# Fourth and fifth key-weight pieces by DMA transposes on two queues

## The chip, the cores and the metric

The kernel runs on one core of a Trainium2 chip. The metric is the device time of one execution in microseconds (us); the figure compared is the median of the timed runs. One further execution is taken under the hardware profiler, and the profile and the trace come from it.

## What is computed

The reference is one transformer layer over 2048 tokens of width 640: layer normalisation, linear attention with 32 heads of width 20, and a SiLU feed-forward part of width 1728, each with its residual. The change touches only the keys. Cut to what matters:

```python
x = A_x                                             # 1 x 2048 x 640, bf16
qkv = layernorm(x) @ wqkv                           # 640 x 1920: q, k, v
pk = einsum("bhsd,hdf->bhsf", k, w_phi)             # per head, 20 x 20
phi_k = concat([softmax(pk), softmax(-pk)])         # likewise phi_q from q
kv, z = sum over tokens of phi_k * v, phi_k
h = x + (phi_q @ kv / (phi_q @ z + 1e-6)) @ wo
out = h + silu(layernorm(h) @ w1) @ w2
```

Since the head map `w_phi` follows directly on the key projection, the kernel multiplies the two weights once (`Wfk` = key weights times the block-diagonal `w_phi`) and then projects each token tile with `Wfk`. For that product TensorE needs the key weights transposed: the tile `wTk`.

## The kernel before

The tokens lie in 16 tiles of 128. The width 640 is cut in C = 5 pieces of 128, and so are the key weights: piece c is rows 128c to 128c + 127 of the key columns. Persistent tiles hold the tokens (`X`), the weights, and the results in between; PSUM is one tile `mm` of eight banks, and the number behind `@` in the order is the bank that a step writes.

The order of all work is written out by hand in the string `ORDER`: each word is a step (`wt.3` is the function `op_wt(3)`), and each engine and each DMA queue takes its own instructions strictly in the order in which the words give them. A tile framework puts in the waits between engines. Two queues issue DMAs: SP (SyncE), which does nothing else, and ACT (ScalarE), which also computes. In the steps for loads a last letter `a` means ACT and `s` means SP.

The steps around the change, with their lines in the profile:

- `lx.a.b` loads token tiles a to b - 1 into `X`, `lk.a.b` key pieces a to b - 1 into `wk`, `lv.a.b` value pieces into `wv`, `lo.a.b` output weights, `lp` the head map (all issued at L236).
- `wm.n` are matmuls on constants ahead of the first data (L268).
- `wt.c` transposes key piece c on TensorE, five 128 x 128 transposes into PSUM (L322); `wc.c` copies the result into `wTk`, on VectorE (L169) or ScalarE (L171).
- `fk.c` multiplies piece c of `wTk` with the head map (six matmuls, L337), `fc.c` copies the product to `Wfk`, on ScalarE (L171).
- `st.t` takes the statistics of token tile t on VectorE (L273, L274), `rs` turns them into scale and offset on GpSimd, `xn.t` normalises (L297 on VectorE, L302 on ScalarE), `xt.t` transposes the tile on TensorE (L308) and `xc.t` copies it, for tiles 0 to 3; for the other twelve `xd.t` does both by a DMA transpose on SP (L315).
- `kp.t` and `vp.t` project token tile t with `Wfk` and with `wv` (ten matmuls each, L370; the pieces 0 to 4 are read one after the other).
- `ta` loads ScalarE's table for the exponential (L264).
- `lq.c` brings a piece of the query weights transposed by a DMA transpose on SP (L251). The step `lt.c` (L254) does the same for a key piece, and the order of before doesn't use it.

In the order of before SP issues: token tile 1, key pieces 0 to 3 one by one, then X[2:4], X[8:12], value pieces 0 to 2, value pieces 3 and 4, X[4:8], X[12:16], output weights. ACT issues X[0:1], the head map and key piece 4 and then goes on to compute. TensorE's order in the opening is `wm`, `wt.0`, `wm`, `wt.1`, `fk.0`, `wt.2`, `wt.3`, `fk.1`, `fk.2`, `wt.4`, `fk.3`, `xt.0`, `fk.4`, `xt.1`, `kp.0`, `kp.1`, `vp.1`, `xt.2`, `vp.0`, `vp.2`, `xt.3`, `kp.2`, `kp.3`.

Of the kernel before, what the change touches and what calls it, by code (L numbers as in the profile page):

```python
# [22 lines left out]
WHERE = {t: (g, i) for g, ts in enumerate(GROUPS) for i, t in enumerate(ts)}  # L23

ORDER = """
mk mo lx.0.1.a lk.0.1.s lp.a lx.1.2.s lk.4.5.a wm.512@7 wm.512@7 wm.512@7 wm.512@7 wm.512@7 wm.512@7
wm.512@7 wm.512@7 wt.0@0 lk.1.2.s ta wc.0.a wm.256@2 wm.256@2 wm.256@2 wm.256@2 wm.256@2 wm.256@2 wt.1@1 wc.1.a st.0 rs.0.1
ph.v fk.0@2 fc.0.a st.1 lk.2.3.s wt.2@4 wc.2.v lk.3.4.s wt.3@5 wc.3.v fk.1@6 fc.1.a rs.1.2 fk.2@0 fc.2.a
lx.2.4.s xn.0.v lx.8.12.s wt.4@4 wc.4.v lv.0.3.s fk.3@2 fc.3.a xt.0@5 xn.1.v xc.0.v st.2 fk.4@6 fc.4.a
rs.2.3 lv.3.5.s mc.0 xt.1@4 xc.1.a st.9 st.8 rs.8.10 lx.4.8.s st.3 rs.3.4 kp.0@0 ke.0 xn.2.a kp.1@2 ke.1  # L30
lx.12.16.s vp.1@6 st.10 xt.2@5 vp.0@0 xc.2.a xn.9.a vc.0.a vp.2@2 st.11 lo.2.5.s xn.3.v xt.3@4 xc.3.a
rs.10.12 xn.8.a vc.2.a vc.1.a kp.2@0 ke.2 st.4 xd.9 st.5 kp.3@4 lo.0.2.s ke.3 rs.4.6 vp.3@2 xn.11.v vp.9@6
# [38 lines left out]
def kernel(  # L71
# [11 lines left out]
    nc = tc.nc  # L83

    P = nc.NUM_PARTITIONS
    T = 16
    D = 640
# [46 lines left out]
    wTk = first.tile([P, C, D], BF16, name="wTk")  # L134
# [116 lines left out]
        nc.sync.dma_start_transpose(wTq[:, :, c * P : (c + 1) * P], A_wqkv[c * P : (c + 1) * P, 0:D])  # L251

    def op_lt(c, q="s"):
        nc.sync.dma_start_transpose(wTk[:, :, c * P : (c + 1) * P], A_wqkv[c * P : (c + 1) * P, D : 2 * D])  # L254

    def op_lo(a, b, q="s"):
        dma(q, wo[:, a:b, :], A_wo[a * P : b * P].rearrange("(c p) n -> p c n", p=P))
# [500 lines left out]
```

## Time and profile before

| what | us |
|---|---|
| timed runs, median of 3 | 236.51 (236.49 to 236.56) |
| the profiled execution | 236.35 |
| its span, first to last instruction | 234.4 |
| TensorE busy | 230.5 (98%) |
| VectorE busy | 133.5 (57%) |
| ScalarE busy | 114.5 (49%) |
| GpSimd busy | 95.4 (41%) |

The span lies within the profiled execution; the 1.95 us between them are before the first and after the last instruction. In the profile's rows PE is TensorE, DVE VectorE, ACT ScalarE, POOL GpSimd; SPq and ACTq are the DMA issues of a queue. `out<-in` names the tiles written and read, xN is the number of instructions in a row, and all times count from the start of the span.

### The profile page before, as it was taken

Reading aid. Unit: us, or ns where it says so; the run is one execution under the profiler, and the core shown is the slowest. Engines: PE = TensorE matmul, PEld = TensorE weight load, DVE = VectorE, ACT = ScalarE, POOL = GpSimd, SP = SyncE. Lnnn points to the kernel's source line nnn. Section 1 sums busy time; section 2 is a strip of 40 time slices with the busy share of each in tenths; the row PEclk is TensorE's granted clock in tenths of the full one; section 3 lists DMA queues with packets and bytes.
Section 4 is the critical chain, followed back from the end, with each engine's and each line's share of the span. In section 5 each row is a group of like instructions: output and inputs, shape, how many; then the busy total and the mean of one; then the engine's idle time right before and its main releaser. Section 6 shows DMA issues by size and latency. Waiting matters only on the chain.

```text
span 234.4 us, 6307 instructions
## 1 busy us (share of the span) xinstructions
PE 230.5 (98%) x2674; PEld 148.4 (63%) x2674; DVE 133.5 (57%) x249; ACT 114.5 (49%) x171; POOL 95.4 (41%) x190
## 2 busy tenths in 40 slices
PE   8999999999999999999999999999999999999995
PEld 4777777776554556876645455556776865566662
DVE  3999999999968899788956641301341310001132
ACT  3789996885857776742244536260040015613000
POOL 7485798997904455765285123141040000000000
PEclk9999999999999999999999999999999999999999
DMA  7967758839101375325823202123212300000112
GB/s 203 381 234 147 82 112 110 182 64 350 37 3 31 59 176 148 59 49 98 142 55 61 56 3 55 30 57 63 88 24 57 106 27 5 0 3 2 54 34 81
DMA packets 44844, 20.67 MB, mean 88 GB/s; under 512 B 34448, under 2 KB 44304, under 8 KB 44816
## 3 DMA queue, kind: packets, MB, share of 16 engines
q1 hardware_dynamic: 43728, 19.88, 36.1%
q10 hardware_dynamic: 1088, 0.39, 0.8%
q8 instruction: 21, 0.34, 0.6%
q14 instruction: 7, 0.06, 0.1%
HBM read 9.61 MB, written 2.62 MB: 52 GB/s over the span
## 4 chain that ended last, share of the span: by engine, by line
PE 98%; ACT 1%; DVE 0%; issue 0%
PE mm L691 24%; PE mm L645 24%; PE mm L370 19%; PE mm L457 10%; PE mm L566 9%; PE mm L504 3%; PE mm L268 2%; PE mm L427 2%; PE mm L337 1%; PE mm L655 1%; PE mm L704 1%; ACT EqT L479 1%; PE mm L322 1%; PE mm L308 0%; DVE ob L721 0%
## 5 line engine op out<-in xcount | busy, mean ns | idle before, releaser
L691 PE MATMUL mm<-w,shT 128*128 128x320 bf16 (+2 forms) x416 | 58.7, 299 | 0.0
L645 PE MATMUL mm<-HnT,w 128*128 128x512 bf16 (+1 forms) x325 | 58.6, 337 | 0.0
L691 PEld LDWEIGHTS <-shT 128*128 128x128 bf16 x416 | 39.6, 98 | 17.2 <-issue 1.1
L667 ACT ACTIVATE shT<-mm 128x1024 bf16<-128x1024 f32 (+2 forms) x29 | 27.6, 963 | 44.6 <-PE mm L645 43.1
L712 DVE TENSOR_TENSOR ob<-mm,X 128x640 bf16<-128x640 f32 x15 | 12.3, 819 | 62.3 <-PE mm L691 59.3
L645 PEld LDWEIGHTS <-w 128*128 128x128 bf16 x325 | 31.4, 98 | 23.2
L370 PEld LDWEIGHTS <-XnT 128*128 128x128 bf16 x320 | 30.8, 98 | 12.0
L414 POOL TENSOR_TENSOR Ek<-Ek,Sk 128x1280 bf16<-128x1280 bf16 (+2 forms) x15 | 32.9, 2217 | 4.0 <-DVE Sk L406 4.0
L539 POOL TENSOR_TENSOR o<-u,rd 128x320 bf16<-128x320 f32 x28 | 19.9, 727 | 22.9 <-DVE rd L533 16.4
L583 ACT ACTIVATE sq<-X 128x640 bf16<-128x640 bf16 x16 | 11.7, 732 | 28.3 <-DVE X L575 27.2
L566 PE MATMUL mm<-wo,ot 128*128 128x320 bf16 x160 | 23.9, 299 | 0.3 <-ACT EqT L479 0.3
L457 PE MATMUL mm<-XnT,Wfq 128*128 128x512 bf16 x100 | 23.8, 380 | 0.0
L370 PE MATMUL mm<-wv,XnT 128*128 128x320 bf16 x160 | 23.7, 299 | 0.0
L370 PE MATMUL mm<-Wfk,XnT 128*128 128x320 bf16 x160 | 23.5, 299 | 0.0
L395 ACT ACTIVATE Ek<-mm 128x640 bf16<-128x640 f32 x32 | 20.5, 714 | 6.0 <-PE mm L370 5.1
L403 DVE TENSOR_REDUCE Sk<-Ek 128x64 f32<-128x1280 bf16 x16 | 23.2, 1452 | 0.3 <-ACT Ek L395 0.3
L479 ACT ACTIVATE EqT<-mm 128x1024 bf16<-128x1024 f32 (+1 forms) x24 | 19.7, 879 | 4.9 <-PE mm L457 4.8
L575 DVE SCALAR_TENSOR_TENSOR X<-mm,X 128x640 bf16<-128x640 f32 x16 | 13.0, 818 | 15.4 <-PE mm L566 15.1
L566 PEld LDWEIGHTS <-ot 128*128 128x128 bf16 x160 | 15.7, 98 | 7.3 <-issue 0.2
L273 DVE BATCH_NORM_STATS2 stats<-X 128x6 f32<-128x320 bf16 x32 | 13.6, 467 | 3.8 <-DMA X<-in_A_x_dram 3.8
L457 PEld LDWEIGHTS <-Wfq 128*128 128x128 bf16 x100 | 9.1, 98 | 9.3
L525 DVE TENSOR_TENSOR u<-mm,w 128x672 f32<-128x672 f32 x16 | 13.7, 857 | 1.2 <-DVE w L523 0.3
(78 smaller groups left out, 204.3 us busy)
## 6 DMA issues: line engine op xcount, KB each, us to landing
out_dram<-ob SPq DMA_DIRECT2D x15, 160.0 KB, 1.8
w<-in_B_w_dram SPq DMA_DIRECT2D x6, 360.0 KB, 4.5
X<-in_A_x_dram SPq DMA_DIRECT2D x3, 640.0 KB, 7.8
w<-in_B_w_dram SPq DMA_DIRECT2D x5, 320.0 KB, 5.8
wk<-in_A_wqkv_dram SPq DMA_DIRECT2D x4, 160.0 KB, 4.2
wv<-in_A_wqkv_dram SPq DMA_DIRECT2D x1, 480.0 KB, 6.4
wo<-in_A_wo_dram SPq DMA_DIRECT2D x1, 480.0 KB, 9.7
w<-in_B_w_dram SPq DMA_DIRECT2D x1, 480.0 KB, 4.6
```

The costliest lines, as they stand in the source:

```text
L370: nc.tensor.matmul(ps[:, half, 0:320], tok(XnT[t // GT], t)[:, c, :], W[:, c, half * 320 : (half + 1) * 320], start=(c == 0), stop=(c == C ...
L395: nc.scalar.activation(Ek[:, s, :].rearrange("p (a n) -> p a n", a=2), tl["kp", t][:, :, 0:320], AF.Exp, scale=1.0 - 2.0 * s,)
L403: nc.vector.tensor_reduce(Sk[:], tl["ek", t][:].rearrange("p s (h f) -> p (s h) f", f=DH), axis=AX.X, op=ALU.add,)
L414: nc.gpsimd.tensor_tensor(Ek3[:, 0:n], Ek3[:, 0:n], Sk[:, 0:n].unsqueeze(2).to_broadcast([P, n, DH]), op=ALU.mult,)
L457: nc.tensor.matmul(tl["qp", g, i][:, k, :], Wfq[:, c, r * P : (r + 1) * P], XnT[g][:, c, :], start=(c == 0), stop=(c == C - 1),)
L479: nc.scalar.activation(E[:, s, rs[0] : rs[-1] + 1, :], tl["qp", g, i][:, 0 : len(rs), :], AF.Exp, scale=1.0 - 2.0 * s,)
L525: nc.vector.tensor_tensor(u[:], A[1][:, :, :, 0:21], w[:].unsqueeze(3).to_broadcast([P, 4, 8, 21]), op=ALU.mult,)
L539: (nc.vector if eng == "v" else nc.gpsimd).tensor_tensor(tl["o", t][:, a * 320 : (a + 1) * 320].rearrange("p (h f) -> p h f", f=DH), tl["u ...
L566: nc.tensor.matmul(ps[:, half, 0:320], tl["ot", t][:, c, :], wo[:, c, half * 320 : (half + 1) * 320], start=(c == 0), stop=(c == C - 1),)
L645: nc.tensor.matmul(ps[:, i * W : (i + 1) * W], w1[:, c, fc * P : (fc + 1) * P], HnT[g][:, c, 0:W], start=(c == 0), stop=(c == C - 1), skip ...
L667: nc.scalar.activation(sh[:, a:b], tl["up", g, k][:, 0 : b - a], AF.Silu)
L691: nc.tensor.matmul(ps, shT[g][:, fc * W + i * P : fc * W + (i + 1) * P], w2[:, fc, a:b], start=first and fc == 0, stop=last and fc == FC - ...
```

## The change

The fourth and the fifth key piece (c = 3 and 4) are no longer loaded into `wk`, transposed by `wt` and copied by `wc`. Instead `lt.4` on ACT's queue and `lt.3` on SP's queue bring them from DRAM by DMA transposes straight into their columns of `wTk`, in the places of the order where `lk.4.5.a` and `lk.3.4.s` stood. The step `lt` gets a choice of queue. With the loads go two `wt` steps (ten TensorE transposes) and two `wc` steps (two VectorE copies); all other steps stay as they are and in the same order.

```diff
-mk mo lx.0.1.a lk.0.1.s lp.a lx.1.2.s lk.4.5.a wm.512@7 wm.512@7 wm.512@7 wm.512@7 wm.512@7 wm.512@7
+mk mo lx.0.1.a lk.0.1.s lp.a lx.1.2.s lt.4.a wm.512@7 wm.512@7 wm.512@7 wm.512@7 wm.512@7 wm.512@7
 wm.512@7 wm.512@7 wt.0@0 lk.1.2.s ta wc.0.a wm.256@2 wm.256@2 wm.256@2 wm.256@2 wm.256@2 wm.256@2 wt.1@1 wc.1.a st.0 rs.0.1
-ph.v fk.0@2 fc.0.a st.1 lk.2.3.s wt.2@4 wc.2.v lk.3.4.s wt.3@5 wc.3.v fk.1@6 fc.1.a rs.1.2 fk.2@0 fc.2.a
-lx.2.4.s xn.0.v lx.8.12.s wt.4@4 wc.4.v lv.0.3.s fk.3@2 fc.3.a xt.0@5 xn.1.v xc.0.v st.2 fk.4@6 fc.4.a
+ph.v fk.0@2 fc.0.a st.1 lk.2.3.s wt.2@4 wc.2.v lt.3.s fk.1@6 fc.1.a rs.1.2 fk.2@0 fc.2.a
+lx.2.4.s xn.0.v lx.8.12.s lv.0.3.s fk.3@2 fc.3.a xt.0@5 xn.1.v xc.0.v st.2 fk.4@6 fc.4.a
 rs.2.3 lv.3.5.s mc.0 xt.1@4 xc.1.a st.9 st.8 rs.8.10 lx.4.8.s st.3 rs.3.4 kp.0@0 ke.0 xn.2.a kp.1@2 ke.1
...
     def op_lt(c, q="s"):
-        nc.sync.dma_start_transpose(wTk[:, :, c * P : (c + 1) * P], A_wqkv[c * P : (c + 1) * P, D : 2 * D])
+        (nc.sync if q == "s" else nc.scalar).dma_start_transpose(wTk[:, :, c * P : (c + 1) * P], A_wqkv[c * P : (c + 1) * P, D : 2 * D])
```

## The prediction

> **What bounds the kernel now.** I began with the share of busy time and with the chain of waits, because a small change to the opening is only worth what it takes off that chain. The page says that TensorE (PE) has practically no idle time, and the chain says where its first microseconds go (start, length, instructions; L322 transposes pieces of the key weights, L337 folds them, L308 transposes tokens, L370 projects):
>
> ```profile
> PE 230.5 (98%) x2674; PEld 148.4 (63%) x2674; DVE 133.5 (57%) x249; ACT 114.5 (49%) x171; POOL 95.4 (41%) x190
> 7.02 0.56 PE mm L322 x10
> 7.58 0.80 PE mm L337 x12
> 8.37 0.28 PE mm L322 x5
> 8.65 0.32 PE mm L337 x6
> ...
> 10.04 4.19 PE mm L370 x30
> 14.24 0.28 PE mm L308 x5
> 14.52 2.72 PE mm L370 x20
> 17.23 0.28 PE mm L308 x5
> ```
>
> The reader is to see two things. The transposes that go are on this chain: `wt.2` and `wt.3` together take 0.56 us, `wt.4` 0.28 us. And from 10.04 us on PE runs one matmul after the other, 30 of them in 4.19 us, so a late arrival there is paid in full and nothing later gives it back.
>
> The second view is the timeline of the two issuing queues, SP (SyncE) and ACT (ScalarE), for the opening:
>
> ```profile
> 1.74 1.49 SPq L236 DMA_DIRECT2D wk<-in_A_wqkv_dram  x3
> 3.83 0.80 SPq L236 DMA_DIRECT2D X<-in_A_x_dram  x2
> 4.88 0.93 SPq L236 DMA_DIRECT2D wv<-in_A_wqkv_dram  x2
> ...
> 1.70 0.56 ACTq L236 DMA_DIRECT2D wk<-in_A_wqkv_dram  x1
> 2.28 1.28 ACT L264 ACT_TABLE_LOAD   x1 [2.28 <-issue]
> ...
> 4.97 0.69 ACT L171 COPY wTk<-mm 128x640 bf16<-128x640 bf16 x1 [1.20 <-PE mm L322]
> ```
>
> The third load of the first row is the fourth key piece; behind it on SP stand the token tiles X[2:4] and X[8:12] (both in the row at 3.83) and the whole of the value weights (4.88). The fifth key piece is issued on ACT at 1.70.
>
> The third view is the list of DMA issues with the time from issue to landing (last column), asked for the opening and for a few single issues:
>
> ```profile
> wv<-in_A_wqkv_dram SPq DMA_DIRECT2D x1, 480.0 KB, 6.4
> ...
> X<-in_A_x_dram SPq DMA_DIRECT2D x1, 320.0 KB, 4.0
> wv<-in_A_wqkv_dram SPq DMA_DIRECT2D x1, 320.0 KB, 6.8
> ...
> wk<-in_A_wqkv_dram ACTq DMA_DIRECT2D x1, 160.0 KB, 4.3
> X<-in_A_x_dram SPq DMA_DIRECT2D x1, 640.0 KB, 5.7
> wo<-in_A_wo_dram SPq DMA_DIRECT2D x1, 320.0 KB, 3.3
> L251 SPq DMA_TRANSPOSE wk<-in_A_wqkv_dram x5: 1219/1232/1275, 21.7 to 41.6; - x5
> ...
> DMA to landing us min/median/max: 2.8/3.1/4.2
> ```
>
> From these come the landings of before: X[2:4] at 3.83 + 4.0 = 7.8 us, X[8:12] (issued about 4.25) at 10.0, the first three value pieces at 4.88 + 6.4 = 11.3, the last two (issued about 5.35) at 12.15. The last two rows belong to L251, which brings the query weights later by the same kind of transpose, out of the same array and in the same size: the issuing queue is held 1.23 us and the data stand 2.8 to 4.2 us after the issue, 3.1 in the median.
>
> **The change part by part.** *What PE loses.* `wt.3` is half of the 0.56 us and `wt.4` is 0.28, so 0.56 us leave the chain if everything else is ready. Not all of that can be had: the folds between them also wait for copies. I take 0.5 us as the most that the change can bring.
>
> *What the vector engine loses.* Two copies out of PSUM:
>
> ```profile
> L169 DVE COPY wTk<-mm x3: 480/490/491, 7.3 to 8.7; 128x640 bf16<-128x640 bf16 x3
> ```
>
> That is 2 x 0.49 us, before 9.2 us. It lets the first two normalised tiles be ready early enough to follow PE; it isn't a gain of its own, since PE is the chain.
>
> *The transpose on ACT.* It takes 1.23 us of the queue where the load took 0.56, so the table load that follows starts at about 2.95 and not 2.28, and ends, with the 0.2 us behind it, near 4.4. The next work on ACT is the copy at 4.97, which had waited 1.20 us for PE. I cost it at nothing; that copy's idle time hides it, with some 0.5 us left over.
>
> *The transpose on SP, and the wait.* Here lies the change. `lt.4` goes through ACT's queue, `lt.3` comes later in the order and goes through SP's. The framework in which the kernel is written keeps DMA transposes of two queues from being in flight together: it lets the later one wait for the landing of the earlier. Every transpose of before is on SP's queue, so no row of before can show such a wait; but that SP's queue does stand still for a landing, with all behind it, is seen in the list of its waits:
>
> ```profile
> SPq L236 <- DMA X<-in_A_x_dram: 0.6, 1, 0.6
> ```
>
> So SP would stand before `lt.3` until the ACT transpose has landed. The Trainium skill, page "DMA: Bandwidth & Descriptors", section "Silent corruption: two transposing streams in flight at once", says that transposes issued from SP and from ACT are two streams, and that the later stream's first transpose must wait for the full completion count of the earlier one. No run here shows it yet; with that rule the sum is the one below, without it that of the first rival.
>
> When does SP go on? The bounds are worked out from the rows: earliest 1.70 + 2.8 = 4.5 us (the quickest of the later transposes, which had the DMA engines nearly to themselves); as the load that it replaces, 1.70 + 4.3 = 6.0; latest about 6.7, that load's time plus the 0.67 us by which the transpose's issue is longer. I take 6.0 and 0.1 us for the release, 6.1, since that load stood in the same queue behind the same two transfers. A landing below 4.5 us has no row.
>
> Behind the wait, in order:
> - `lt.3` is issued at 6.1, holds SP until 7.35 and lands at 6.1 + 3.1 = 9.2 us (the DMA engines have run dry by then, so the quiet row is the nearest).
> - X[2:4] is issued at 7.4, 3.6 us later than before, and lands, on drained engines, as the other 320 KB load did, in 3.3 us: 10.7 us instead of 7.8, 2.9 us later.
> - The rest follows at the rate of before, when the engines were just as backlogged: from X[2:4] to X[8:12] 2.2 us, to the first value pieces 3.5, to the last 4.35. That gives 12.9, 14.2 and 15.05 us.
>
> Who waits for these, from the timelines of PE and the vector engine (the projection `vp.1`, the statistics `st.9`, the normalisation `xn.3`):
>
> ```profile
> 12.72 1.52 PE L370 MATMUL mm<-wv,XnT 128*128 128x320 bf16 x10
> 11.07 0.88 DVE L273 BATCH_NORM_STATS2 stats<-X 128x6 f32<-128x320 bf16 x2
> ...
> 16.31 0.39 DVE L297 TENSOR_SCALAR xn<-X,MV,RS 128x640 bf16<-128x640 bf16 x1
> ```
>
> First stall: the fold `fk.3`. Without `wt.3` and `wt.4` it could start at 8.65 - 0.45 = 8.2 us; `lt.3` lands at 9.2, so PE stands 1.0 us and is then 0.5 late, and `kp.0` starts at about 10.55 instead of 10.04. Second stall: `vp.1`, the first reader of the value weights. PE reaches it at 10.55 + 20 x 0.136 = 13.3 us; pieces 0 to 2 are there at 14.2 (6 matmuls, to 15.0) and pieces 3 and 4 at 15.05 (4 matmuls, 0.54 us), so it ends at 15.6 instead of 14.24: 1.35 us late. This stall contains the first; they aren't added. Third: `st.9` needs X[8:12] at 12.9 instead of starting at 11.07, 1.8 us late; that row of vector work runs without gaps up to `xn.3`, which ended at 16.70, 0.5 us ahead of its reader on PE at 17.23. So `xt.3` comes 1.3 us late by this path, the same as by the other. X[4:8] and X[12:16] land under 3 us later and are read far enough behind. The query transposes and stores later on SP find it idle. The sum is therefore +1.35 us, with the 0.56 us of PE already inside it (it was spent waiting).
>
> On the profiled execution of before, 236.35 us, this gives 237.7; that execution lay 0.16 us under the median of the runs, 236.51, so I forecast 237.8. By the bounds for SP's release the price moves one for one: at 4.6 us it is about zero (`vp.1` would end at 14.1), at 6.8 it is +2.05. About 0.2%, or 0.47 us, is what a measurement of this kernel can tell from no change.
>
> **The rivals.** *No wait, and the change does what it says.* SP issues `lt.3` at about 2.8, holds the queue 0.7 us longer than the load did, and both transposes land by 7.0 us (2.8 + 4.2, the slowest row), ahead of the 8.2 us at which they are needed. X[2:4] and the value weights come at most 0.7 us later, 12.85 us for the last piece, while `vp.1` would need it at 12.2 + 0.8 = 13.0. The gain is the 0.5 us of the chain: 236.0 us. For it speaks that the chain holds just these instructions; against it that the two transposes write one tile through two queues. Chance 0.08.
>
> *The wait exists but ends early.* If the ACT transpose lands by 5 us, the price is between -0.1 and +0.4 us: 236.4 to 236.9. Only the quiet rows speak for it, and the opening isn't quiet: its load of the same size took 4.3 us. Chance 0.1.
>
> *The stall slows PE's clock as well.* The rows of the matmuls show two speeds, 512 columns in 0.446 us at the start (8 in 3.57 us) and in 0.216 us later (20 in 4.32 us):
>
> ```profile
> 0.83 3.57 PE L268 MATMUL mm<-const-bfloat16-1.0 128*128 128x512 bf16 x8 [0.83 <-PEq L742]
> 140.92 4.32 PE mm L645 x20
> ```
>
> PE got to the higher speed only after some 5.5 us of work (the row at 7.02 is the first at the full rate, ten transposes in 0.56 us). If standing idle for 1.0 and then 0.9 us within 6 us takes it back, a second rise of up to 5.5 us at half speed costs up to 2.7 us more, estimated from those rows: 239.2 to 240.5. Against it: the stalls are short, and the one PE stall of 1.95 us in before is followed by matmuls at the full rate:
>
> ```profile
> 86.30 1.95 ACT EqT L479 x2
> 88.25 0.04 issue
> 88.29 1.52 PE mm L566 x10
> ```
>
> Chance 0.08. [...]
>
> **How the numbers follow.** The forecast (wait, release between 5.0 and 6.8 us) has 0.74 and spans 236.9 to 238.6. The range 236.4 to 239.0 adds the early release and some of the later landings that a busier opening could give; it leaves out the gain (0.08) and most of the clock case (0.08). Faster by over 0.2% is the better half of the no-wait case, 0.05. Within 0.2% (236.04 to 236.98) fall the rest of that case and most of the early release, 0.12. Slower is the remainder, 0.83.
>
> **What would show it.** Right: on SP a gap between the load of the third piece (near 2.7 us) and a DMA transpose of about 1.23 us that starts near 6.1, whose end of waiting is the landing of the ACT transpose; X[2:4] issued near 7.4; PE waiting about 1 us ahead of an L337 for a DMA of wTk and nearly 1 us ahead of the first L370 that reads wv; the vector engine waiting for X near 11 and 12 us; then the same pace as before. Wrong: the transpose on SP issued by 3 us (then the first rival), wTk landing ahead of 8 us, or matmuls of 320 columns slower than 0.136 us after 10 us. If the SP transpose starts at 6.1 but PE is on time at `vp.1`, my rate of landing was too slow.

## The result and the profile after

The changed kernel takes 239.5 us (median of five executions) against 236.51 us before; the ratio is 1.0131, with a 95% interval of 1.0118 to 1.0144. It is 3.0 us slower. The profiled execution has a span of 237.9 us, 3.5 more than that of before (234.4).

PE is still the busiest engine and is busy as long as before; its share falls because it waits:

```profile
PE 230.4 (97%) x2664; PEld 148.0 (62%) x2664; DVE 132.8 (56%) x247; ACT 114.9 (48%) x171; POOL 95.4 (40%) x190
```

The timelines of the two issuing queues, SP and ACT, and the row of SP's list of waits that belongs to the new transpose:

```profile
1.71 0.90 SPq L236 DMA_DIRECT2D wk<-in_A_wqkv_dram  x2
6.86 1.28 SPq L254 DMA_TRANSPOSE wTk<-in_A_wqkv_dram  x1
8.20 1.05 SPq L236 DMA_DIRECT2D X<-in_A_x_dram  x2
9.29 0.96 SPq L236 DMA_DIRECT2D wv<-in_A_wqkv_dram  x2
...
1.72 1.30 ACTq L254 DMA_TRANSPOSE wTk<-in_A_wqkv_dram  x1
...
SPq L254 <- DMA wTk<-in_A_wqkv_dram: 4.2, 1, 4.2
```

SP issues nothing between 2.6 and 6.86 us: it waits 4.2 us for the ACT transpose, and X[2:4] is issued at 8.20 us (3.83 before), the value weights at 9.29 (4.88). By the end of this wait the DMA engines have run empty: their share and GB/s, the last two figures of these rows of the windows, fall to nothing (in before the same two microseconds have 1.19 and 0.92, 414 and 358 GB/s):

```profile
6.00:7.00 1.00, 0.78 (x13) 0.58 (x10) 0.96 (x4) 0.50 (x1) 0.80 (x2) 1.00 0.04 11
7.00:8.00 1.00, 0.77 (x11) 0.59 (x11) 0.58 (x2) 0.88 (x3) 0.00 (x0) 1.00 0.00 0
```

The landings, from the list of DMA issues:

```profile
wv<-in_A_wqkv_dram SPq DMA_DIRECT2D x1, 480.0 KB, 5.9
...
X<-in_A_x_dram SPq DMA_DIRECT2D x1, 320.0 KB, 3.9
wv<-in_A_wqkv_dram SPq DMA_DIRECT2D x1, 320.0 KB, 6.3
...
wTk<-in_A_wqkv_dram ACTq DMA_TRANSPOSE x1, 5.1
```

The ACT transpose stands at 1.72 + 5.13 = 6.85 us, the moment at which SP goes on. The chain of waits leads from there straight to `vp.1`:

```profile
1.72 5.13 DMA wTk<-in_A_wqkv_dram
...
6.86 1.28 SPq L254
...
9.29 5.86 DMA wv<-in_A_wqkv_dram
...
15.19 1.58 PE mm L370 x10
```

PE's own waits for data, from its timeline, and then the chain of waits further on:

```profile
9.80 0.49 PE L337 MATMUL mm<-phb,wTk 128*128 128x140 bf16 x6 [1.17 <-DMA wTk<-in_A_wqkv_dram]
...
15.19 1.58 PE L370 MATMUL mm<-wv,XnT 128*128 128x320 bf16 x10 [1.15 <-DMA wv<-in_A_wqkv_dram]
...
16.77 0.28 PE mm L308 x5
...
70.53 0.24 PE mm L504 x18
70.76 0.57 issue
71.34 0.33 PE mm L504 x22
71.67 2.91 PE mm L457 x13
```

The reader is to see two losses. `xt.2` (L308), which follows `vp.1`, starts at 16.77 us instead of 14.24: 2.53 us late. The other stands far from the change: the first matmuls of L504, in before one row without a gap,

```profile
67.95 0.42 PE mm L504 x40
68.37 2.91 PE mm L457 x13
```

break off after 18 of 40 and go on 0.57 us later, with nothing that the profile shows to wait for. The L457 behind them starts at 71.67 us instead of 68.37, 3.3 late. Some 0.2 us more are lost later; together that is the 3.5 us of span.

### The profile page after: what moved, and what is told of

It is laid out like the page before. It is cut to its first block, busy times and chain, and to the rows that moved or that the text cites. A ratio compares the mean times of both kernels' runs of the same rounds, so it can differ in the third digit from the quotient of the medians.

```text
span 237.9 us, 6285 instructions
## 1 busy us (share of the span) xinstructions
PE 230.4 (97%) x2664; PEld 148.0 (62%) x2664; DVE 132.8 (56%) x247; ACT 114.9 (48%) x171; POOL 95.4 (40%) x190
## 4 chain that ended last, share of the span: by engine, by line
PE 88%; DMA 5%; DVE 2%; POOL 1%; SPq 1%; ACT 1%; issue 1%; ACTq 0%; DVEq 0%
PE mm L691 23%; PE mm L645 23%; PE mm L370 17%; PE mm L457 9%; PE mm L566 7%; PE mm L504 2%; DMA wv<-in_A_wqkv_dram 2%; DMA wTk<-in_A_wqkv_dram 2%; PE mm L427 2%; PE mm L655 1%; PE mm L704 1%; POOL o L539 1%; ACT EqT L479 1%; DVE u L525 1%; DVE u L528 1%; PE mm L337 1%
## 5 line engine op out<-in xcount | busy, mean ns | idle before, releaser
L457 PE MATMUL mm<-XnT,Wfq 128*128 128x512 bf16 x100 | 23.8, 380 | 0.0
L457 PEld LDWEIGHTS <-Wfq 128*128 128x128 bf16 x100 | 9.0, 98 | 9.3
```

What stands on the lines that cost most here:

```text
L457: nc.tensor.matmul(tl["qp", g, i][:, k, :], Wfq[:, c, r * P : (r + 1) * P], XnT[g][:, c, :], start=(c == 0), stop=(c == C - 1),)
```

## The experiments

The theory at this point: SP's wait for the other queue's transpose is the main price, paid at `vp.1`. Its rival: the transposes are slow and costly in the crowded opening, wait or no wait. And the gap at L504 needs a cause of its own.

**Both transposes on ACT's queue.** One stream, so nothing on SP waits.

```diff
-lx.1.2.s lt.4.a wm.512@7 ... wc.2.v lt.3.s fk.1@6
+lx.1.2.s lt.4.a lt.3.a wm.512@7 ... wc.2.v fk.1@6
```

> Both key transposes on ACT's queue, one behind the other, SP free of them: the one stream removes the wait of SP (4.2 us in the profile of the change). Theory (the price is SP standing still, with the loads of tokens and value weights behind it): X[2:4] is issued near 3.2 us, vp.1 is not late, and the time falls back to 236.0 to 236.7 us. Rival (the transposes themselves are slow in the opening, and the folds wait for them): the second transpose, issued near 3.0 us, lands near 8.5 us or later, fk.3 waits, and the time stays above 237.5. ACT is held 1.3 us longer ahead of the table load, so the copy wc.0 starts near 5.9 us instead of 4.97; that may cost 0.2 us at the first fold.

Measured: 237.63 us, ratio 1.0036 (1.0022 to 1.0050). X[2:4] is issued at 3.85 us and the wait of SP before X[2:4] for the other queue is gone; `vp.1` starts at 13.15 us with nothing to wait for. So taking the wait away brought back 1.9 us of the 3.0. But the theory's range was missed by 0.9 us, and the time even lies above the rival's bound of 237.5, though the rival's sign isn't there: no fold waits for a transpose. What is lost is lost in two places:

```profile
7.66 0.45 PE L322 MATMUL mm<-ident,wk 128*128 128x128 bf16 x5 [0.69 <-DMA wk<-in_A_wqkv_dram]
...
69.42 0.33 PE L504 MATMUL mm<-KVBD,EqT 32*128 32x44 bf16 x22 [0.77 <-issue]
```

The third key piece, a plain load on SP, lands late (PE waits 0.69 us for it), and the gap at L504 is there again, at the same instruction.

**Only the fifth piece, on ACT.** The fourth is loaded, transposed and copied as before.

```diff
-lx.1.2.s lk.4.5.a wm.512@7 ... lx.8.12.s wt.4@4 wc.4.v lv.0.3.s
+lx.1.2.s lt.4.a wm.512@7 ... lx.8.12.s lv.0.3.s
```

> Only the fifth piece by a transpose on ACT; the fourth is loaded, transposed on TensorE and copied as before, so there is no second queue and no wait. Theory: 236.1 to 236.6 us (0.28 us of TensorE transposes less, nothing else moved); the ACT transpose lands near 6.9 us, well before fk.4 reads it. Rival (one slow transpose in the opening is enough, because it crowds the loads): the third key piece and X[2:4] land later, and the time is 237 us or more.

Measured: 237.2 us, ratio 1.0029 (1.0018 to 1.0040). Here the rival is right: with a single transpose, no wait between queues and 0.28 us less for PE, the kernel is still slower. PE waits for the second and the third key piece, and the DMA engines say why (from the windows: PEclk, share of the DMA engines, GB/s stand last; the last row is of the kernel before):

```profile
5.90 0.45 PE L322 MATMUL mm<-ident,wk 128*128 128x128 bf16 x5 [0.87 <-DMA wk<-in_A_wqkv_dram]
...
7.89 0.89 PE L322 MATMUL mm<-ident,wk 128*128 128x128 bf16 x10 [1.12 <-DMA wk<-in_A_wqkv_dram]
...
5.00:6.00 1.00, 0.13 (x3) 0.10 (x3) 0.96 (x3) 0.13 (x1) 0.59 (x1) 1.00 1.06 171
...
8.00:9.00 1.00, 1.00 (x17) 0.83 (x17) 0.61 (x2) 0.00 (x0) 0.00 (x0) 1.00 1.06 425
...
5.00:6.00 1.00, 1.00 (x6) 0.55 (x4) 1.00 (x3) 0.67 (x1) 0.76 (x1) 1.00 1.09 384
```

While the transpose is in flight the engines are full and move 171 GB/s; in the kernel before, with plain loads alone, they are as full in the same microsecond and move 384 (and 425 here three microseconds later). A share above 1 says that the times of an engine's packets overlap. There is no gap at L504 here; this kernel has ten TensorE instructions fewer ahead of it, the two before have twenty (a weight load and a matmul for each transpose left out).

**The hold alone.** The kernel before, with SP held by a 64-byte copy that reads what the copy `wc.1` writes.

```diff
+    def op_hs():
+        nc.sync.dma_start(junk[0:1, :], wTk[0:1, 0, P : P + 32])
...
-lx.2.4.s xn.0.v lx.8.12.s
+hs lx.2.4.s xn.0.v lx.8.12.s
```

> The kernel before, with SP alone held: a 64-byte copy that reads a corner of wTk after the copy wc.1 has written it (about 7.4 us) stands in SP's queue ahead of X[2:4]. All loads, TensorE transposes and copies of before stay. Theory: X[2:4] is issued near 7.9 us (8.20 in the changed kernel), the value weights stand near 14.9 us, vp.1 waits, and the kernel takes 2 to 3 us more than before, 238.5 to 239.5 us, without any key transpose. Rival (it is the transposes' own slowness that costs): 236.5 to 237.2 us.

Measured: 237.86 us, ratio 1.0059 (1.0037 to 1.0081), from the executions at full clock, which stand between 237.5 and 237.9 us but for one of 239.4. That is 1.2 us, where 2 to 3 were expected; it lies between the ranges of theory and rival. The profiled execution itself took 241.18 us with a granted clock of 0.992, and its timeline of PE shows what happened to it:

```profile
14.63 0.97 PE L374 MATMUL mm<-wv,XnT 128*128 128x320 bf16 x6 [1.75 <-DMA wv<-in_A_wqkv_dram]
16.61 1.11 PE L374 MATMUL mm<-wv,XnT 128*128 128x320 bf16 x4 [1.01 <-DMA wv<-in_A_wqkv_dram]
17.52 0.74 PE L312 MATMUL mm<-ident,xn 128*128 128x128 bf16 x5
18.05 3.93 PE L374 MATMUL mm<-wv,XnT 128*128 128x320 bf16 x20
...
18.00:22.00 4.00, 4.00 (x27) 2.62 (x25) 3.90 (x12) 2.21 (x3) 2.37 (x7) 0.73 0.52 149
```

SP went on later here than at full clock (X[2:4] is issued at 8.13 us). After the two stalls five transposes take 0.74 us instead of 0.44, twenty matmuls 3.93 us instead of 2.88, and the granted clock of that window is 0.73. The next run shows the same kernel without that.

**The hold again.** The same kernel.

> The same kernel as the hold alone (SP held until the copy wc.1 at about 7.4 us, nothing else changed), once more, because its profiled execution had TensorE at about half speed from 16.6 us for some 4 us after two stalls of 1.75 and 1.0 us, while its other executions, with full clock, were only 1.2 us over the kernel before. Question: what the profile of an execution at full clock shows. Theory (the hold shifts the loads, and PE's loss is where vp.1 waits): vp.1 is late by 1.2 us, with the value weights standing near 15 us, and 237.5 to 238.0 us. Rival (the loads stand as late as in the other profile, 14.6 and 16.6 us, and something gives time back later): vp.1 late by 2.5 us or more and a lateness that shrinks afterwards.

Measured: 237.86 and 237.92 us at full clock, and 241.23 and 241.41 us at 0.993 and 0.992; over all four the ratio is 1.0130 (1.0074 to 1.0186). The profile is of one at full clock:

```profile
7.48 1.05 SPq L237 DMA_DIRECT2D X<-in_A_x_dram  x2
...
13.76 1.59 PE L374 MATMUL mm<-wv,XnT 128*128 128x320 bf16 x10 [1.02 <-DMA wv<-in_A_wqkv_dram]
```

In this execution the copy that ends the hold was done at 6.8 us and X[2:4] was issued at 7.48, not at 8.13 as in the other profile. `vp.1` waits 1.02 us for the value weights, `xt.2` is 1.1 us late, and the span is 235.9: nothing is given back later. So the hold alone, without any key transpose, makes `vp.1` wait, and 1.1 us is its price when X[2:4] is issued at 7.48. In the other profile, with the issue at 8.13, the first value pieces were there at 14.6 us and the last at 16.6, later still than the last in the changed kernel (16.1), whose issue stood at 8.20. The price of a hold as long as the changed kernel's is seen in that one execution only, and there the lost clock is mixed into it.

**A shorter hold.** The copy reads what `wc.0` writes.

```diff
-        nc.sync.dma_start(junk[0:1, :], wTk[0:1, 0, P : P + 32])
+        nc.sync.dma_start(junk[0:1, :], wTk[0:1, 0, 0:32])
```

> The hold alone, but ended by the copy wc.0 (about 5.7 us) and not by wc.1 (7.4 us): X[2:4] is issued near 6.3 us, 1.8 us earlier than in the hold alone. Theory: the price falls one for one until vp.1 is on time; from 1.2 us at full clock it goes to nothing, 236.4 to 236.9 us. Rival (any hold of SP that lets the DMA engines run dry costs about the same): 237.4 us or more.

Measured: 236.66 us, ratio 1.0009 (0.9997 to 1.0020): no difference.

```profile
6.37 1.05 SPq L237 DMA_DIRECT2D X<-in_A_x_dram  x2
...
12.86 1.55 PE L374 MATMUL mm<-wv,XnT 128*128 128x320 bf16 x10
```

X[2:4] comes 2.5 us later than in the kernel before and `vp.1` is only 0.14 us late, with no wait that the profile lists. SP's queue had over 2 us to spare; by these two profiles the price begins near an issue at 6.4 us and rises about one for one, to 1.1 us at 7.48.

**The gap at L504.** The changed kernel with ten matmuls on constants where the ten transposes stood.

```diff
-wt.2@4 wc.2.v lt.3.s fk.1@6 ... lv.0.3.s fk.3@2
+wt.2@4 wc.2.v lt.3.s wm.128@7 (five times) fk.1@6 ... lv.0.3.s wm.128@7 (five times) fk.3@2
```

> The changed kernel with ten 128-column matmuls on constants in TensorE's order where the ten transposes stood (five ahead of fk.1, five ahead of fk.3), so that TensorE's instruction stream has its old length and every later instruction its old place. They run while TensorE waits for wTk anyway. Question: of the 3.5 us of span, 2.5 are there at vp.1, and 0.7 appear at the first matmuls L504 near 70.5 us, as 0.57 us in which nothing in the profile is waited for. Theory A (that gap comes from the place in the instruction stream): it is gone, and the time is 238.7 to 239.1 us. Theory B (it comes from when things happen): it stays, 239.3 to 239.7 us.

Measured: 239.09 us, ratio 1.0103 (1.0089 to 1.0117), just below the changed kernel's interval though PE does more and SP went on later still in its profile, at 7.40 us. The gap is gone:

```profile
71.42 0.42 PE mm L504 x40
```

Theory A holds as far as it goes: the gap follows the place in TensorE's instruction stream. All three kernels here with twenty instructions fewer ahead of L504 have it (the changed one, both transposes on ACT, and the transpose ahead of the head map further down, with 0.74 us), none with ten fewer or as many as before.

**Filled stream and one queue.** The first experiment with the same ten matmuls.

```diff
-lt.4.a lt.3.a wm.512@7 ... wc.2.v fk.1@6 ... lv.0.3.s fk.3@2
+lt.4.a lt.3.a wm.512@7 ... wc.2.v wm.128@7 (five times) fk.1@6 ... lv.0.3.s wm.128@7 (five times) fk.3@2
```

> Both transposes on ACT's queue, as in the first experiment, and in addition the ten filling matmuls in TensorE's order that removed the 0.57 us gap from the changed kernel. The first experiment stood 1.5 us of span over the kernel before: 0.43 at vp.1 and 0.77 us as the gap at the first L504. Theory (the two parts add, and the gap goes with the place in the instruction stream): the gap is gone and the time is 236.6 to 237.1 us. Rival (the gap comes from the late start): it stays, 237.4 us or more.

Measured: 237.24 us, ratio 1.0030 (1.0019 to 1.0040), 0.14 us over the theory's range. The gap is gone (L504 is one row of 40 in 0.42 us), but in this profile the opening is later: `kp.0` starts at 10.84 us, not at 10.42. The median is 0.4 us below that of the first experiment, but the two intervals overlap (1.0022 to 1.0050 there), so what the filling is worth here isn't clear of the noise. Only the missing gap is shown.

**The transpose ahead of the head map.**

```diff
-lk.0.1.s lp.a lx.1.2.s lt.4.a
+lk.0.1.s lt.4.a lx.1.2.s lp.a
```

> The changed kernel, with the head map's load and the transpose of the fifth piece exchanged in ACT's queue: the transpose is issued at about 1.2 us, ahead of the 640 packets of 40 bytes of the head map and half a microsecond earlier. Theory A (the transpose landed 5.1 us after its issue because it stood behind the head map in the queue): it lands near 4.8 us, SP goes on near 4.9 us instead of 6.85, and the time falls by 1.5 to 2 us, to about 237.7. Theory B (its own small packets share the DMA engines with the loads of the opening and come last whatever stands ahead): it lands near 6.2 us, the time falls by no more than the half microsecond, 238.8 to 239.4. The head map comes later and may hold up fk.0 by some tenths.

Measured: 239.42 us, ratio 1.0138 (1.0109 to 1.0167). Theory B, and a little worse than it said:

```profile
1.21 1.29 ACTq L254 DMA_TRANSPOSE wTk<-in_A_wqkv_dram  x1
...
6.90 1.30 SPq L254 DMA_TRANSPOSE wTk<-in_A_wqkv_dram  x1
```

Issued half a microsecond earlier and with only the first token tile ahead of it in its queue, the transpose lands 5.7 us after its issue and SP goes on at 6.90 us, as late as before. So it isn't the head map alone that delays it. The second key piece now lands at 6.7 us and the head map at 7.4; PE waits 1.4 us for each, and its granted clock is 0.50 in the window from 8 to 12 us. Five of the six executions have a granted clock of 0.986 to 0.993, so this kernel's time holds that price too.

**One transpose, late, on SP.** The kernel before with the fifth piece brought by a transpose behind X[2:4].

```diff
-lx.1.2.s lk.4.5.a wm.512@7 ... lx.2.4.s xn.0.v lx.8.12.s wt.4@4 wc.4.v lv.0.3.s
+lx.1.2.s wm.512@7 ... lx.2.4.s lt.4.s xn.0.v lx.8.12.s lv.0.3.s
```

> The kernel before with one transpose only, of the fifth piece, on SP behind X[2:4]: no second queue, no load of that piece early, no wt.4 and wc.4. wTk's last columns are needed near 9.2 us; the transpose is issued near 4.2 us. Theory: it stands by 8.5 us, 0.28 us of TensorE time is saved, X[8:12] and the value weights come up to 0.8 us later and just in time: 236.2 to 236.6 us, the one form that could beat the kernel before. Rival (a transpose in the opening crowds the loads, as with the one on ACT): 236.9 to 237.4 us.

Measured: 235.98 us, ratio 0.9987 (0.9974 to 1.0001).

```profile
3.91 1.30 SPq L254 DMA_TRANSPOSE wTk<-in_A_wqkv_dram  x1
...
12.44 1.52 PE L370 MATMUL mm<-wv,XnT 128*128 128x320 bf16 x10
```

In this profile `vp.1` starts 0.28 us earlier than in the kernel before, as much as the transposes of `wt.4` took. Once more, for the interval:

> One transpose, of the fifth piece, on SP behind X[2:4], once more for its interval, beside the next kernel: 235.8 to 236.2 us, 0.3 to 0.5 below the kernel before.

Measured: 236.07 us, ratio 0.9986 (0.9973 to 0.9999).

```profile
12.69 1.58 PE L370 MATMUL mm<-wv,XnT 128*128 128x320 bf16 x10
```

Here `vp.1` starts only 0.03 us earlier than in the kernel before, and the span is the same, 234.4 us. The medians of both runs lie 0.46 us below the kernel before, the ratios 0.3 us; the first interval holds 1, the second ends just short of it. It is the one version that seems to beat the kernel before, and only by about as much as can be told from no difference.

**Both transposes on SP.**

```diff
-lx.1.2.s lk.4.5.a wm.512@7 ... wm.256@2 (six times) wt.1@1 ... wc.2.v lk.3.4.s wt.3@5 wc.3.v fk.1@6
+lx.1.2.s wm.512@7 ... wm.96@2 (sixteen times) wt.1@1 ... wc.2.v lt.3.s fk.1@6
-lx.2.4.s xn.0.v lx.8.12.s wt.4@4 wc.4.v lv.0.3.s
+lx.2.4.s lt.4.s xn.0.v lx.8.12.s lv.0.3.s
```

> Both transposes on SP's one queue, behind the three loaded key pieces: the fourth piece ahead of X[2:4], the fifth behind it; the six 256-column matmuls on constants before wt.1 become sixteen of 96 columns, which is the same work and keeps TensorE's instruction stream at its old length. No wait between queues, no small packets ahead of the key loads. Theory: the short hold showed that SP has over 2 us to spare before vp.1 is late; both pieces stand in time (near 7.5 and 8.8 us), the 0.56 us of TensorE transposes is saved and 235.7 to 236.0 us is reached. Rival: the fourth piece lands after 8.2 us or X[8:12] and the value weights come too late, 236.4 us or more.

Measured: 237.71 us, ratio 1.0044 (1.0030 to 1.0058). The rival. The folds have what they need, `kp.0` starts at 9.53 us, half a microsecond early, and then `vp.1` waits:

```profile
14.47 1.62 PE L370 MATMUL mm<-wv,XnT 128*128 128x320 bf16 x10 [1.91 <-DMA wv<-in_A_wqkv_dram]
...
7.00:8.00 1.00, 0.82 (x14) 0.49 (x11) 0.97 (x5) 1.00 (x3) 0.23 (x2) 1.00 1.37 137
```

The value weights were issued at 6.48 us, 1 us ahead of those in the shorter hold (7.46), and yet stood 1.5 us after them, at 14.4 instead of 12.86. Between 7 and 8 us the share of the DMA engines is 1.37 and they move 137 GB/s. One of the six executions ran at a granted clock of 0.986 and took 241.94 us. One transpose late in the opening fits; one early on ACT's queue didn't, nor do two on SP.

## Why the prediction was wrong

The direction and the mechanism were right, and the rows that were to show it are there: the gap on SP, the first L337 waiting about 1 us for wTk (1.17), `vp.1` waiting about 1 us for wv (1.15), X[2:4] late. The size was wrong: +1.3 us forecast, +3.0 measured, outside the range.

- *The change on ACT at nothing:* right. The first copy starts at 4.97 us as before.
- *The wait:* right, 4.2 us. The Trainium skill, page "DMA: Bandwidth & Descriptors", section "Silent corruption: two transposing streams in flight at once", asks for it, and the trace agrees: SP's transpose starts at 6.86 us, the moment at which the ACT transpose stands. No run tells this reason from another, that the two transposes write one tile; but the kernel before fills the tile `wk` from both queues without such a wait.
- *When SP goes on:* the first step that failed. I priced the transpose as the plain load in its place, 4.3 us, and took 6.1 us with 6.7 as the latest. It took 5.13 us in this profile, close to that latest, and 5.7 to 5.9 in the five other profiles with a transpose early on ACT's queue; SP went on at 6.86. That is 0.76 us of the miss at `vp.1`. Why it stands so late is open: the transpose ahead of the head map was as late, while one issued on SP at 2.65 us stood 3.8 us later. Nor are the DMA engines full to the end: from 6.4 us on they move nothing.
- *The landings behind the wait:* nearly right. From the issue of X[2:4] to the first value pieces I took 6.8 us; it was 6.95, and the last pieces came 0.9 us behind those. With the end of `vp.1` this makes 0.4 us more than forecast. The holds without a transpose ahead needed 6.2 to 6.5, so `lt.3`, which runs just ahead of these loads, may cost them 0.5 to 0.7 us. Put together from the hold at 7.48 (1.1 us), 0.72 for the issue at 8.20 and this, that is 2.3 to 2.5 us; at `xt.2`, 2.53 were measured. It is an account from single profiles and not a measurement, and in the other profile of the hold the last pieces came 2.0 us behind the first without any transpose.
- *A term at nothing:* the second step that failed, the gap at L504, 0.57 us in the row and 0.7 at the instruction behind it. I had counted the transposes that go as time alone and not as places in the instruction stream. By my own price for a release at 6.8 us, +2.05, the first step alone would have given about 238.6 us, inside the range; this gap and the 0.4 us of the landings carried the time out of it.
- *The three stalls at `vp.1`, `fk.3` and `st.9`, not added:* right. `st.9` started at 13.83 us instead of 11.07, and its path brought no more than `vp.1` did.
- *The clock rival:* I gave it 0.08. One of the five executions of the changed kernel ran at 0.993 and took 240.39 us. The Trainium skill, page "TensorE: Matmul & The Clock Gate", section "Why this matters for your kernels", puts the limit at a gap of about 3 us; the hold alone lost its clock after stalls of 1.75 and 1.01 us in its profiled execution, so the trace doesn't agree, and the measurement decides. One stall alone did not take it in the profiles: after the 1.91 us of both transposes on SP the granted clock stays at 1.00, and so it does after the changed kernel's 1.17 and 1.15, which lie 4 us apart. What I had put against this rival was misread: in the row of 1.95 us at 86.30 it is ScalarE that works, while PE has other matmuls and is idle for 0.27 us:

```profile
86.10 1.52 PE L566 MATMUL mm<-wo,ot 128*128 128x320 bf16 x10
87.56 0.47 PE L504 MATMUL mm<-KVBD,EqT 32*128 32x44 bf16 x40
88.29 1.52 PE L566 MATMUL mm<-wo,ot 128*128 128x320 bf16 x10 [0.27 <-ACT EqT L479]
```

- *No wait, and the change does what it says* (236.0 us), and *the wait ends early:* neither is what happens. Without the wait, on one queue, two transposes cost 0.7 to 1.2 us in three kernels.

What stays open: what TensorE waits for in the gap at L504. Shown is that it follows the number of instructions ahead of it. The traces hold one row that fits: a DMA queue which the profile calls `q8 instruction` moves 21 pieces of 16 KB in the course of the kernel. In the three profiles with the gap, TensorE goes on 2.65 to 2.71 us after the start of the latest such transfer; in the other ten, 2.73 us or more had passed since it when TensorE came to the same matmul, and there is no pause. That reads like a wait for instructions, but no run changed these transfers alone, so it isn't shown. Nor was it tried to let the two queues' transposes overlap; the wait was removed only by putting both on one queue.

## What to carry to other kernels

A transfer that must wait for another queue's transfer holds its whole queue: price what stands behind it, from the slack of each, not the transfer itself. Replacing a load by a DMA transpose in a stretch where the DMA engines are full takes time from the other loads there, so put it where they have time to spare, or keep the TensorE transposes, which here cost 0.28 us for each piece. By the ratios one such edit, placed late, came out 0.3 us ahead, hardly clear of the noise, and two on the same queue 1.0 us behind: both draw on the same slack.

## What the runs showed of the hardware

- A DMA transpose of 160 KB from DRAM takes engine time from the loads beside it: between 5 and 6 us the DMA engines were full at 171 GB/s with one in flight, and at 384 without. It stood 5.1 to 5.9 us after an issue at 1.2 to 1.7 us on ACT's queue (the plain load in its place 4.3), 3.8 to 4.4 after an issue at 2.6 to 4.6 us on SP's, and 2.9 to 3.0 behind the wait, with the engines empty.
- Taking twenty TensorE instructions out of the opening made a gap of 0.57 to 0.77 us at one instruction 60 us later; ten filling matmuls removed it.
- PE's clock can fall after stalls of 1.75 and 1.01 us that lie 1 us apart (granted clock 0.73 in the window behind, execution 241.18 us). In the profile of the same kernel with one stall of 1.02 us it didn't (237.86 us).
